# The turned rows six partitions apart, and low-rank sums with the tokens as the stationary operand

## The chip, the cores and the metric

The kernel runs on one core of one Trainium2 chip. The metric is the time of one execution on the device in microseconds, the median of three runs. Below, TensorE multiplies matrices into PSUM, VectorE, ScalarE and GpSimd do elementwise work, and SyncE issues the DMAs.

## The reference

Three stages follow each other, for 4 batches of 768 tokens with 384 channels.

1. A complex linear recurrence per head (8 heads of 48 channels): `S = (a_re + i a_im) * S + k v`, with `a` cut to a magnitude of 0.999, and `y = q S_re`.
2. A first MoE: `u = x + V'(U'x)`, where U (768x32) and V (32x768) mix tokens with rank 32; then `u + relu(u @ w_ch1) @ w_ch2` with 1536 hidden channels.
3. A second MoE of the same size, whose `u` is `x + Re(FFT2(x))`, normalised per token.

```python
h = xt @ U @ V                      # xt: channels x tokens
u = x + h.transpose(0, 2, 1)
ch = np.maximum(u @ w_ch1, 0.0) @ w_ch2
return (u + ch).astype(np.float32)
```

## The kernel before

**Attention.** A batch is cut into 6 chunks of 128 tokens, numbered 0 to 23 over the four batches. A pair of chunks is loaded with channels on partitions, as 16 groups of 8 heads. VectorE and ScalarE form decays and phases there (the functions `squares` to `gains`), and `rotations` writes q and k, scaled and turned by their phases, into QK: 128 partitions of (channel group x, head h), with the real or imaginary part z and the third i of a head's 48 channels as free axes. For the scores the 96 rows of a head (16 x, 2 z, 3 i) must lie on 96 partitions. `move` (line 316) does this by DMA: six per chunk, each taking QK's 128 partitions for one (z, i) to 16 partitions of QT, which are neighbours (`QT[p0 : p0 + 16]`). From QT and QK TensorE then makes the scores (`scores`, L325), masked by VectorE (L328); the keys turned back by an identity product (`turned`, L332), copied by ScalarE with `by_head` (L335); the sums with the values (`summed`, L343), which give y and the running state; and x, the output of the stage.

**The low-rank mix.** `low_rank` (line 384) multiplies, for each chunk of tokens, U's 128x32 part, repeated four times to 128 columns (three rounded copies and one of what rounding leaves), as the stationary operand with x's 128 tokens by 384 channels as the moving one:

```python
T.matmul(zp, f32(ust[:, c].rearrange("p a r -> p (a r)")), xt[b, c], start=c == 0, stop=c == NC - 1)
```

Six of these add up to zp. ScalarE rounds it to zst (L1028), VectorE replaces 32 of its rows by what the rounding left (L1030). V is then the second factor, once towards u with channels on partitions (`mixed`, L415) and once straight onto the MoE's sums (`extra1`, L449). In the trace an f32 matmul stands as two records, and each has its own weight load.

**The MoE.** For each batch and half a batch (g), `first_product` makes hp for 12 groups of hidden channels (f), ScalarE and VectorE split relu(hp) into hh and hl, and the second product adds onto acc. In the program hp is numbered through: hp_0 opens batch 0, hp_24 batch 1, hp_48 batch 2.

**What sets the order.** The attention of all batches and the first MoE of batches 0 to 2 are written as streams of steps, each with an engine, a duration and what it waits for. `planned` merges them into one order per engine before the program runs, and that order is fixed. PLACES holds a number per kind of step and batch that moves it ahead or back. Where the planner sees TensorE idle it puts in `warm_up` matmuls on constants, 128x256 before hp_0 (L609) and 128x128 behind it (L612). `rank_words` prepares U and V from 64-bit words, `mixing` holds the low-rank steps, `moves` the moves, `word_loads` the MoE's weight loads, which share three staging buffers with the turned keys. All DMAs of these stand on SyncE's one queue, in the planner's order. From batch 3's first MoE on, the order is written by hand, with the Fourier stage beside it.

## Time and profile before

| what | value |
| --- | --- |
| median of 3 runs (lowest, highest) | 863.51 us (861.82, 863.71) |
| the profiled execution | 863.16 us, its span 861.4 us |
| TensorE, VectorE, ScalarE, GpSimd busy | 93%, 73%, 52%, 4% of the span |
| granted clock of TensorE, mean | 0.997 of full speed |
| bytes over DMA | 83.06 MB, mean 96 GB/s |

The busy share of an engine is over the whole span, so stages with other limits are mixed in it; times within the trace count from the start of the span. Fillers count as busy time of TensorE.

### The profile page before, as it was taken

How to read it: one execution, taken by the hardware profiler on the slowest of the kernel's cores; microseconds unless marked ns; L12 is line 12 of the kernel's file. 1: busy time of each engine (PE TensorE's matmuls, PEld its weight loads, DVE VectorE, ACT ScalarE, POOL GpSimd, SP SyncE). 2: the span in 40 equal slices, each digit the busy share in tenths (PEclk: the TensorE clock that was granted, in tenths of full speed). 3: DMA queues.
4: the chain of work that ended last, by engine and by line, in shares of the span. 5: the costliest groups of instructions: out<-in, count | busy, mean ns of one | idle time of the engine just before them, and what ended most of it. 6: DMA issues, size and time to landing. Idle time of an engine off the chain costs nothing.

```text
span 861.4 us, 17279 instructions
## 1 busy us (share of the span) xinstructions
PE 799.0 (93%) x6947; PEld 542.1 (63%) x6947; DVE 627.7 (73%) x1304; ACT 450.6 (52%) x845; POOL 36.1 (4%) x79
## 2 busy tenths in 40 slices
PE   0298999999899999999999999999999999999996
PEld 0187755567766677666776665666666666666663
DVE  6989689998779977988965846657485657645652
ACT  7976598798868679758733342142224123311210
POOL 1001000010000000000003200001010100000000
PEclk9999999999999999999999999999999999999999
DMA  9539933588392594359386120103010300000000
GB/s 357 68 67 127 299 108 95 136 160 197 71 200 89 140 201 112 120 125 187 84 133 222 47 74 1 38 1 102 1 47 1 101 29 1 29 1 28 1 29 32
DMA packets 47353, 83.06 MB, mean 96 GB/s; under 512 B 5600, under 2 KB 36576, under 8 KB 47264
## 3 DMA queue, kind: packets, MB, share of 16 engines
q1 hardware_dynamic: 45984, 77.94, 37.6%
q0 software_dynamic: 1280, 3.93, 1.4%
q8 instruction: 56, 0.92, 0.5%
q14 instruction: 33, 0.27, 0.1%
HBM read 53.39 MB, written 9.44 MB: 73 GB/s over the span
## 4 chain that ended last, share of the span: by engine, by line
PE 75%; ACT 12%; DVE 6%; DMA 4%; issue 2%; SPq 1%; DVEq 0%; ACTq 0%
PE acc L210 10%; PE acc L211 10%; PE hp L105 10%; PE hp L107 10%; PE hp L106 10%; PE acc L224 7%; PE sc L325 4%; PE y L343 3%; PE acc L1083 3%; DMA QT<-QK 3%; ACT ain L101 2%; ACT L97 2%; PE g L343 1%; ACT hh L201 1%; PE z L385 1%
## 5 line engine op out<-in xcount | busy, mean ns | idle before, releaser
L201 ACT ACTIVATE hh<-hp 128x384 f16<-128x384 f32 x192 | 93.5, 489 | 303.5 <-PE hp L107 295.3
L204 DVE SCALAR_TENSOR_TENSOR hl<-hp,hh 128x384 f16<-128x384 f32 x192 | 105.6, 554 | 134.5 <-ACT hh L201 133.7
L210 PE MATMUL acc<-w,hh 128*128 128x384 f16 x576 | 187.7, 326 | 3.6 <-ACT hh L201 3.4
L211 PE MATMUL acc<-w,hh 128*128 128x384 f16 x576 | 187.3, 326 | 0.0
L105 PE MATMUL hp<-u,w 128*128 128x384 f16 x288 | 94.6, 328 | 0.1
L107 PE MATMUL hp<-u,w 128*128 128x384 f16 x288 | 94.5, 328 | 0.0
L106 PE MATMUL hp<-u,w 128*128 128x384 f16 x288 | 94.5, 328 | 0.0
L105 PE MATMUL hp<-n,w 128*128 128x384 f16 x288 | 93.9, 326 | 0.0
L107 PE MATMUL hp<-n,w 128*128 128x384 f16 x288 | 93.9, 326 | 0.0
L106 PE MATMUL hp<-n,w 128*128 128x384 f16 x288 | 93.9, 326 | 0.0
L210 PEld LDWEIGHTS <-hh 128*128 128x128 f16 x576 | 56.3, 98 | 40.4 <-ACT hh L201 6.6
L105 PEld LDWEIGHTS <-w 128*128 128x128 f16 x576 | 56.5, 98 | 37.8 <-issue 0.5
L107 PEld LDWEIGHTS <-w 128*128 128x128 f16 x576 | 56.5, 98 | 37.6 <-issue 0.5
L106 PEld LDWEIGHTS <-w 128*128 128x128 f16 x576 | 56.5, 98 | 36.8 <-issue 0.7
L224 PE MATMUL acc<-w,hl 128*128 128x384 f16 x360 | 77.5, 326 | 0.0
L211 PEld LDWEIGHTS <-hh 128*128 128x128 f16 x576 | 56.4, 98 | 33.1 <-issue 0.4
L325 PE MATMUL sc<-QT 96*128 96x128 f32 x384 | 50.0, 284 | 10.6 <-DMA QT<-QK 9.8
L325 PEld LDWEIGHTS sc<-QT 96*128 96x128 f32 x384 | 47.1, 197 | 13.0 <-issue 11.7
L332 PE MATMUL kp<-ident,QK 128*128 128x128 f32 x120 | 19.8, 292 | 33.6 <-DVE QK L309 31.3
L224 PEld LDWEIGHTS <-hl 128*128 128x128 f16 x360 | 35.2, 98 | 23.6
L1083 PE MATMUL acc<-w,hl 128*128 128x384 f16 x216 | 48.6, 327 | 1.4 <-DVE hl L204 1.4
L97 ACT ACT_TABLE_LOAD x33 | 42.3, 1283 | 1.3 <-PEq L1752 0.7
(264 smaller groups left out, 1414.4 us busy)
## 6 DMA issues: line engine op xcount, KB each, us to landing
QT<-QK SPq DMA_DIRECT2D x144, 129.0 KB, 6.9
stw<-in_w_dram SPq DMA_DIRECT2D x48, 384.0 KB, 5.3
ain<-in_a_dram SPq DMA_DIRECT2D x12, 768.0 KB, 7.0
qkin<-in_qk_dram SPq DMA_DIRECT2D x12, 768.0 KB, 6.9
x1d<-x SPq DMA_DIRECT2D x24, 192.0 KB, 3.4
vin<-in_v_dram SPq DMA_DIRECT2D x18, 192.0 KB, 3.4
lo<-x1d SPq DMA_DIRECT2D x12, 192.0 KB, 3.7
out_dram<-lo SPq DMA_DIRECT2D x12, 192.0 KB, 2.0
```

The costliest lines, as they stand in the source:

```text
L97: ordered(lambda: A.preload_act_table_set(name))
L105: T.matmul(o, ah, bh, start=start, stop=False, skip_group_check=skip)
L106: T.matmul(o, ah, bl, start=False, stop=False, skip_group_check=skip)
L107: T.matmul(o, al, bh, start=False, stop=stop, skip_group_check=skip)
L201: A.activation(hh, hp, AF.Relu)
L204: V.scalar_tensor_tensor(out=hl, in0=hp, scalar=0.0, in1=whole_of(hh), op0=ALU.max, op1=ALU.subtract)
L210: T.matmul(acc[t], hh[:, TSS[t]], w[:, 0, 384:], start=f == 0, stop=False)
L211: T.matmul(acc[t], hh[:, TSS[t]], w[:, 1, 384:], start=False, stop=False)
L224: T.matmul(acc[t], hl[:, TSS[t]], wt[mi, f][:, 0, 384:], start=False, stop=last_step and mi == 1)
L325: T.matmul(ps[:, h, :], q[:, 128:256], q[:, :128], start=True, stop=True)
L343: T.matmul(out[p, hsl], l(h)[:, p], r[:, hsl], start=h == 0 and o + done == 0, stop=h == 7 and o + rest == len(ops) - 1, skip_group_check= ...
L1083: T.matmul(accs[t], hls[n][:, TSS[t]], wt[0, every[n][2]][:, 0, 384:], start=False, stop=False)
```

## The change

`move` sends a (z, i) to the partitions z*3 + i, z*3 + i + 6, and so on: 16 partitions six apart, so that a head's row is x*6 + z*3 + i. `by_head` writes the turned keys in the same row order. U is kept once, as 128x32 in f32, without the rounded copies; its copy on ScalarE moves 192 columns instead of 576, and VectorE's pass for the rest (L705) is gone. `low_rank` now holds the tokens (three 128x128 parts of x) in TensorE, and U's 32 columns move; the sums lie as channels by ranks (zt, 96 columns for three parts). `thrice` has ScalarE copy each part's 32 columns three times beside each other, and `ranks_turned` turns the three 128x96 parts back on TensorE. From there all goes on as before, with 96 rows in place of 128. The planner is given 0.62 instead of 1.0 for a move and 0.25 instead of 0.65 for a chunk's sum, and every number in PLACES is new, so that the order of the planned part is another.

```diff
@@ -314,8 +314,7 @@
         V.tensor_copy(QK[:, :, :, 256:258], ew[m][4][:, :, j : j + 1].unsqueeze(1).to_broadcast([128, 2, 3, 2]))
 
     def move(QT, QK, z, i):
-        p0 = z * 48 + i * 16
-        nc.sync.dma_start(QT[p0 : p0 + 16], QK[:, z, i, :])
+        nc.sync.dma_start(QT[z * 3 + i : 96 : 6], QK[:, z, i, :])
 
     halves = slice(0, 64), slice(64, 128)
 
@@ -332,7 +331,8 @@
             T.transpose(ps[:, i * 128 : (i + 1) * 128], QK[:, z, i, 128:256], ident)
 
     def by_head(ks, ps, z):
-        A.copy(ks[:, :768].rearrange("t (h z x) -> t h z x", h=8, z=2)[:, :, z, :], ps.rearrange("t (x h) -> t h x", h=8))
+        to = ks[:, :768].rearrange("t (h x z i) -> t z h i x", h=8, z=2, i=3)
+        A.copy(to[:, z], ps.rearrange("t (i x h) -> t h i x", i=3, h=8))
 
     def summed(out, ops, done=0, rest=0):
 
@@ -381,23 +381,35 @@
         for n, sign in enumerate((1.0, -1.0)):
             V.tensor_scalar(unread, f32(vst), sign, 0.0, ALU.mult, ALU.max, accum_out=stat("v", 0, n))
 
-    def low_rank(zp, b, c):
-        T.matmul(zp, f32(ust[:, c].rearrange("p a r -> p (a r)")), xt[b, c], start=c == 0, stop=c == NC - 1)
+    def low_rank(zt, b, c):
+        for k in range(3):
+            ks = slice(k * 128, (k + 1) * 128)
+            T.matmul(zt[:, k * 32 : (k + 1) * 32], xt[b, c][:, ks], ust[:, c], start=c + k == 0, stop=c == NC - 1, skip_group_check=True)
+
+    def thrice(zt, b):
+        zx = xpl[0].tile([128, 3, 3, 32], F32, tag="zx", name=f"zx{b}", bufs=1)
+        A.copy(zx, zt.rearrange("d (k r) -> d k r", k=3).unsqueeze(2).to_broadcast([128, 3, 3, 32]))
+        return zx
+
+    def ranks_turned(zp, zx):
+        for k in range(3):
+            x = zx[:, k].rearrange("d n r -> d (n r)")
+            T.matmul(zp[:96, k * 128 : (k + 1) * 128], x, ident, is_transpose=True, start=k == 0, stop=k == 2, skip_group_check=True)
 
     def prelim(b):
 
-        zp = bank(f"z{b}")[:, :DM]
+        zp = bank(f"z{b}")
         for c in range(NC):
-            low_rank(zp, b, c)
+            low_rank(zp[:, DM:], b, c)
             if c % 2:
                 yield
+        zx = thrice(zp[:, DM : DM + 96], b)
+        ranks_turned(zp, zx)
         z = xpl[0].tile([128, DM], F32R, tag="zst", name=f"zst{b}", bufs=2)
-        A.copy(z, zp)
-        V.tensor_tensor(z[64:96], zp[64:96], f32(z[64:96]), ALU.subtract)
+        A.copy(z[:96], zp[:96, :DM])
+        V.tensor_tensor(z[64:96], zp[64:96, :DM], f32(z[64:96]), ALU.subtract)
         zst[b] = z
         yield
-        if parts16[0]:
-            A.activation(zp, zp, AF.Square, accum_out=stat("z", b, 0))
 
     def tokens(xp, b, g, k):
         for t in range(3):
@@ -414,8 +426,8 @@
     def mixed(xp, b, g, k):
         T.matmul(
             xp,
-            zst[b][:, k * 128 : (k + 1) * 128],
-            vst[:, g * 384 : (g + 1) * 384],
+            zst[b][:96, k * 128 : (k + 1) * 128],
+            vst[:96, g * 384 : (g + 1) * 384],
             start=False,
             stop=True,
             skip_group_check=True,
@@ -441,12 +453,12 @@
         for k in range(3):
             piece(k)
             if k == 2 and g == 1 and parts16[0]:
-                A.activation(zst[b], f32(zst[b]), AF.Copy, scale=UP * WP[0] * WP[1])
+                A.activation(zst[b][:96], f32(zst[b][:96]), AF.Copy, scale=UP * WP[0] * WP[1])
             yield
 
     def extra1(b, g, t, acc):
         c = g * 3 + t
-        T.matmul(acc, vst[:, c * 128 : (c + 1) * 128], zst[b], start=False, stop=True)
+        T.matmul(acc, vst[:96, c * 128 : (c + 1) * 128], zst[b][:96], start=False, stop=True)
 
     def added(acc, x, scale):
         if parts16[0]:
@@ -484,39 +496,39 @@
             yield
 
     PLACES = {
-        "squares": (-31, 3, 8, 62, 65, -112, 112, -43, 6),
...
-        "mixing": (25,),
...
+        "squares": (-28, -2, 5, 56, 44, -172, 104, -43, 14),
...
+        "mixing": (20,),
...
         "positive_lows": (-4,),
...
     }
     def planned(streams, sizes):
 
@@ -690,7 +702,7 @@
         def rank_words(x):
             u = x == "u"
             n = 192 if u else 384
-            yield op("A", 0.35 if u else 0.45, f"{x}a", x, holds=[("x1", f"{x}l")])
+            yield op("A", 0.35 if u else 0.45, f"{x}a", x, holds=[("x1", "uh" if u else f"{x}l")])
             w = slot(f"wx{x}")[:, :n]
             steps = word_steps(words_of[x], w)
             steps[0][1]()
@@ -699,10 +711,8 @@
                 steps[k][1]()
             if u:
                 ur = w.rearrange("p (c r) -> p c r", c=NC)
-                yield op("A", 0.6, "uh", "uc")
-                A.copy(ust[:, :, 0:3, :], ur.unsqueeze(2).to_broadcast([128, NC, 3, 32]))
-                yield op("V", 0.3, "ul", "uh")
-                V.tensor_tensor(ust[:, :, 3, :], ur, f32(ust[:, :, 0, :]), ALU.subtract)
+                yield op("A", 0.4, "uh", "uc")
+                A.copy(ust, ur)
             else:
                 zs = slice(int(x[1]) * 384, int(x[1]) * 384 + 384)
                 yield op("A", 0.45, f"{x}h", f"{x}c")
@@ -913,7 +923,7 @@
                     if c > 2:
                         before += [f"y{c - 3}"] + ([f"fe{c - 3}"] if turned_too(c - 3) else [])
                     at_end = (z, i) == (1, 2)
-                    yield op("S", 1.0, f"qt{c}" if at_end else f"qt{c}.{z}{i}", *before)
+                    yield op("S", 0.62, f"qt{c}" if at_end else f"qt{c}.{z}{i}", *before)
                     if z == i == 0:
                         QTs[c] = qk_tile("QT", *divmod(c, NC))
                     move(QTs[c], QKs[c], z, i)
@@ -1015,24 +1025,26 @@
         def mixing(b):
             for c in range(NC):
                 n = b * NC + c
-                if b == 0:
-                    yield op("P", 0.65, f"z{n}", f"x{n}", "ul", holds=[("hid", "zs0")] if c == 0 else [])
-                else:
-                    yield op("P", 0.65, f"z{n}", f"x{n}", f"x{b * NC + NC - 1}", holds=[("ms", f"zs{b}")] if c == 0 else [])
+                ready = [f"x{n}", "uh"] if b == 0 else [f"x{n}", f"x{b * NC + NC - 1}"]
+                yield op("P", 0.25, f"z{n}", *ready, holds=[("hid" if b == 0 else "ms", f"zs{b}")] if c == 0 else [])
                 if c == 0:
-                    banks["z", b] = bank(f"z{b}", phid if b == 0 else pms)[:, :DM]
-                low_rank(banks["z", b], b, c)
-            zp = banks["z", b]
-            yield op("A", 0.42, f"zh{b}", f"z{b * NC + NC - 1}", *([f"ex{b - 2}.1.2"] if b > 1 else []))
+                    banks["z", b] = bank(f"z{b}", phid if b == 0 else pms)
+                low_rank(banks["z", b][:, DM:], b, c)
+            zp = banks["z", b][:96, :DM]
+            yield op("A", 0.4, f"zx{b}", f"z{b * NC + NC - 1}", *([f"zt{b - 1}"] if b else []))
+            zx = thrice(banks["z", b][:, DM : DM + 96], b)
+            yield op("P", 0.35, f"zt{b}", f"zx{b}", "ident")
+            ranks_turned(banks["z", b], zx)
+            yield op("A", 0.42, f"zh{b}", f"zt{b}", *([f"ex{b - 2}.1.2"] if b > 1 else []))
             z = zst[b] = xpl[0].tile([128, DM], F32R, tag="zst", name=f"zst{b}", bufs=2)
-            A.copy(z, zp)
+            A.copy(z[:96], zp)
             yield op("V", 0.5, f"zl{b}", f"zh{b}", "v0l", "v1l")
             V.tensor_tensor(z[64:96], zp[64:96], f32(z[64:96]), ALU.subtract)
             yield op("A", 0.55, f"zs{b}", f"zl{b}")
-            A.activation(zp, zp, AF.Square, accum_out=stat("z", b, 0))
+            A.activation(zp, zp, AF.Square, accum_out=stat("z", b, 0)[:96])
             if b < LATE:
                 yield op("A", 0.5, f"zsc{b}", *[f"mix{b}.{g}.{k}" for g in range(2) for k in range(3)])
-                A.activation(z, f32(z), AF.Copy, scale=UP * WP[0] * WP[1])
+                A.activation(z[:96], f32(z[:96]), AF.Copy, scale=UP * WP[0] * WP[1])
 
         def pieces(b, g, k):
             if (b, g) == (0, 0):
@@ -1476,7 +1488,7 @@
     halfpi = const("halfpi", [128, 1])
     least = const("least", [128, 1])
     most = const("most", [128, 1])
-    ust = const("ust", [128, NC, 4, 32], F32R)
+    ust = const("ust", [128, NC, 32])
     vst = const("vst", [128, S], F32R)
     G.memset(one, 1.0)
     G.memset(stats, 0.0)
```

**SyncE's queue, moves of chunks 2 to 5** (QT_2 to QT_5 are the chunks' tiles, stw_f_z a weight load of the first MoE). Before:

```order
L318 DMA QT_3_532<-QK_3_520 16x8x258 x6
L128 DMA stw_2_0_720<-in_w_dram 128x768
L128 DMA stw_2_1_724<-in_w_dram 128x768
L318 DMA QT_4_796<-QK_4_742 16x8x258 x6
L128 DMA stw_3_0_817<-in_w_dram 128x768
L128 DMA stw_3_1_822<-in_w_dram 128x768
L318 DMA QT_5_825<-QK_5_793 16x8x258 x6
```

And with the change:

```order
L317 DMA QT_3_674<-QK_3_483 16x8x258 x6
L128 DMA stw_2_0_806<-in_w_dram 128x768
L317 DMA QT_4_808<-QK_4_747 16x8x258 x6
L317 DMA QT_5_883<-QK_5_798 16x8x258 x2
L128 DMA stw_2_1_904<-in_w_dram 128x768
L317 DMA QT_5_883<-QK_5_798 16x8x258 x3
L128 DMA stw_3_0_946<-in_w_dram 128x768
L128 DMA stw_3_1_949<-in_w_dram 128x768
L317 DMA QT_5_883<-QK_5_798 16x8x258
```

One weight load has gone from ahead of chunk 4's moves to between chunk 5's, and the last move of chunk 5 stands behind two more.

**TensorE, the opening of batch 1's first MoE** (xp is u before its split, zst1 the low-rank result of batch 1, kp_12 the turned keys of chunk 12, hp_24 the first product). Before:

```order
L404 MATMUL xp_1_0_2_2740<-ident_81,x_8_2366 128x128
L415 MATMUL xp_1_0_2_2740<-vst_89,zst1_2667 128x384
L332 MATMUL kp_12_0_2750<-ident_81,QK2_0_2744 128x128 x3
L332 MATMUL kp_12_1_2757<-ident_81,QK2_0_2744 128x128 x3
L105 LDWEIGHTS w0_255
L105 MATMUL hp_24_2764<-u_1_0_0_2710,w0_255 128x384
```

And with the change (fillers left out):

```order
L416 MATMUL xp_1_0_2_2741<-ident_81,x_8_2400 128x128
L427 MATMUL xp_1_0_2_2741<-vst_89,zst1_2707 128x384
...
L105 LDWEIGHTS w0_252
L105 MATMUL hp_24_2767<-u_1_0_0_2739,w0_252 128x384
L106 LDWEIGHTS w0_252
L106 MATMUL hp_24_2767<-u_1_0_0_2739,w0_252 128x384
```

The key turns of chunk 12 no longer stand ahead of hp_24; they come behind later products.

**TensorE, the low-rank sums of batch 2** (z2; x_12 to x_17 are its chunks of tokens). Before:

```order
L385 MATMUL z2_4007<-x_12_3000,ust_88 128x384
L385 MATMUL z2_4007<-x_13_3133,ust_88 128x384
L385 MATMUL z2_4007<-x_14_3691,ust_88 128x384
L385 MATMUL z2_4007<-x_15_3767,ust_88 128x384
L385 MATMUL z2_4007<-x_16_3886,ust_88 128x384
L385 MATMUL z2_4007<-x_17_3999,ust_88 128x384
```

And with the change:

```order
L387 MATMUL z2_4084<-ust_88,x_12_3234 128x32 x3
L387 MATMUL z2_4084<-ust_88,x_13_3299 128x32 x3
L387 MATMUL z2_4084<-ust_88,x_14_3787 128x32 x3
L387 MATMUL z2_4084<-ust_88,x_15_3869 128x32 x3
L387 MATMUL z2_4084<-ust_88,x_16_3948 128x32 x3
L387 MATMUL z2_4084<-ust_88,x_17_4078 128x32 x3
...
L397 MATMUL z2_4084<-ident_81,zx2_4119 96x128 x3
```

Six matmuls of 384 columns have become eighteen of 32, and three turns come one product later.

## Rows read from the trace of the kernel before

**Rows 1.** The page: busy time of each engine, and TensorE's busy tenths in 40 slices.

```profile
PE 799.0 (93%) x6947; PEld 542.1 (63%) x6947; DVE 627.7 (73%) x1304; ACT 450.6 (52%) x845; POOL 36.1 (4%) x79
...
PE   0298999999899999999999999999999999999996
```

**Rows 2.** Busy time by stretch: from:to, length, engines' busy us, TensorE's clock, DMA.

```profile
0.00:40.00 40.00, 2.44 (x9) 1.65 (x9) 31.80 (x55) 34.27 (x53) 2.21 (x15) 1.00 0.70 219
40.00:108.40 68.40, 63.40 (x864) 54.77 (x865) 56.14 (x95) 44.02 (x83) 4.22 (x10) 1.00 0.79 165
108.40:238.30 129.90, 121.87 (x1248) 84.98 (x1246) 115.22 (x188) 112.72 (x192) 3.25 (x12) 1.00 0.54 129
238.30:463.50 225.20, 223.45 (x2220) 155.26 (x2219) 183.41 (x312) 153.90 (x279) 10.75 (x24) 0.99 0.64 140
463.50:861.40 397.90, 387.81 (x2613) 245.46 (x2612) 241.09 (x657) 105.73 (x241) 15.64 (x18) 1.00 0.11 37
```

**Rows 3.** The chain that ended last, from 78 us on: start, us, what.

```profile
78.79 0.97 DVE QK L309
...
88.40 8.94 DMA QT<-QK
...
97.43 2.02 PE sc L325 x16
```

**Rows 4.** SyncE's queue from 79 us on: start, us, what it issued.

```profile
79.78 3.80 SPq L318 DMA_DIRECT2D QT<-QK  x6
83.69 1.02 SPq L128 DMA_DIRECT2D stw<-in_w_dram  x2
84.81 4.14 SPq L318 DMA_DIRECT2D QT<-QK  x6
```

**Rows 5.** The tile QT: its DMA issues (ns, min/median/max) and their time to landing.

```profile
L318 SPq DMA_DIRECT2D QT<-QK x144: 547/596/1492, 31.4 to 439.7; - x144
...
DMA to landing us min/median/max: 3.1/6.9/9.6
```

**Rows 6.** Stretches with moves alone, and with loads into 128 partitions; the last number is GB/s.

```profile
37.00:39.00 2.00, 0.00 (x0) 0.00 (x0) 1.90 (x3) 1.99 (x2) 0.00 (x0) 1.00 1.15 124
...
14.00:18.00 4.00, 0.00 (x0) 0.00 (x0) 3.00 (x5) 3.89 (x5) 0.00 (x0) 1.00 1.05 393
```

**Rows 7.** The chain again: scores of four heads, y, one batch's sums, key turns.

```profile
261.29 0.89 PE sc L325 x8
...
326.35 0.93 PE y L343 x32
...
337.38 3.87 PE z L385 x12
...
354.08 0.66 PE kp L332 x6
```

**Rows 8.** Groups of instructions by line: out<-in, shapes, count, busy us, mean ns, idle before.

```profile
L97 ACT ACT_TABLE_LOAD x33 | 42.3, 1283 | 1.3 <-PEq L1752 0.7
...
L609 PE MATMUL warm<-ident,mask 128*128 128x256 f16 x210 | 25.6, 281 | 0.0
...
L343 PEld LDWEIGHTS y<-S,QT 96*64 96x64 f32 x640 | 20.3, 138 | 5.3 <-issue 1.8 <-DVE pm L328 1.0 <-DVE wxw L139 0.5
...
L335 ACT COPY k<-kp 128x384 f32<-128x384 f32 x40 | 17.6, 477 | 11.5 <-PE kp L332 8.4 <-PE g L343 3.0
...
L612 PE MATMUL acc<-ident,mask 128*128 128x128 f16 x127 | 8.2, 219 | 0.0
...
L385 PEld LDWEIGHTS z<-x,ust 128*128 128x128 f32 x48 | 8.5, 190 | 4.2
...
L1327 ACT ACTIVATE ach<-ac 97x388 f16<-97x388 f32 x8 | 4.8, 598 | 0.0
```

**Rows 9.** TensorE in order of time before batch 1's first product; idle time in brackets.

```profile
237.49 1.00 PE L332 MATMUL kp<-ident,QK 128*128 128x128 f32 x6 [0.70 <-DVE QK L314]
238.29 0.52 PE L105 MATMUL hp<-u,w 128*128 128x384 f16 x1
```

60 lines of the change are left out of this document (30 added, 30 removed).

## The prediction

> **What bounds the kernel now.** I began with the page: TensorE is busy 799 us of 861.4, and its row of slices is empty only at the start [rows 1]. That busy time holds fillers, matmuls that the planner puts into gaps it foresees: 210 of 25.6 us and 127 of 8.2 us [rows 8]. So I cut the span at three events: the first product of the first MoE (108.4), the first product of batch 1 (238.3) and the first product of batch 3 (463.5), and read each stretch's busy time [rows 2]. Before 40 us TensorE works for 2.4 us. From 40 to 108.4 it is busy for 63.4, of which the 25.6 us of wide fillers are no work. From 108.4 to 238.3 it is busy for 121.9 of 129.9 (8.2 of it narrow fillers), while VectorE is busy for 115.2 and ScalarE for 112.7: all three are nearly full. After 238.3 TensorE idles 1.8 us in 225.2, and then 10.1 in 397.9, most of that at the very end. So up to 238.3 the elementwise work and the transfers set the pace, and behind it TensorE alone. The change acts on both sides, and I price them apart.
>
> **The moves.** Six transfers per chunk carry the turned rows into QT. In the chain of waits that ends last, chunk 5's rotation ends at 79.76, its last move starts landing behind others at 88.40 for 8.94 us, and its scores start at 97.43 [rows 3]. SyncE issues chunk 4's six moves from 79.78, two weight loads at 83.69, chunk 5's six from 84.81 [rows 4]. An issue takes 596 ns at the median, and the fastest move landed 3.1 us after its issue [rows 5]. Where moves run alone they bring 124 GB/s; loads into all 128 partitions bring 393 [rows 6]. One move is 16 x 8 x 258 x 4 = 132,096 bytes, so 132,096 / 124 GB/s = 1.06 us each: twelve need 12.8 us, and they queue behind each other. The change leaves bytes and count as they are and puts a move's 16 partitions six apart instead of side by side. The new time has no row. Above stands today's 1.06; below stands the issue, 0.60, for SyncE cannot hand out moves faster. I take 0.65, near the lower end: the only thing that sets the moves apart from the loads of 393 GB/s is that they end in 16 neighbouring partitions, and that is what is changed.
> [...]
> From the first issue of chunk 4 to the last landing of chunk 5 it is 97.34 - 79.78 = 17.6 us. With the new order (three weight loads among the moves, 0.5 us of issue each by [rows 4]): 12 x 0.65 + 3 x 0.5 + (3.1 - 0.6) = 11.8. **Saved: 5.8.** I take off 0.4, because the last move of chunk 5 now stands on SyncE's queue behind two weight loads that wait for buffers which TensorE frees; whoever is late there delays that move and the scores behind it.
>
> **The chain after the scores.** Behind the last low-rank sum two steps are added before U's product can be copied: ScalarE's threefold copy of 96 columns (no row for its 288 elements a lane; above stands the 0.48 of a 128x384 copy [rows 8], below three quarters of that by its elements, 0.36, and I take 0.45) and three turns, which by the six of 0.66 us [rows 7] cost 0.33. With a hop that is 0.9 us on the path of batch 0, so the first product starts 5.8 - 0.4 - 0.9 = **4.5 us earlier**. The rounding of U loses one vector pass and the copy to ScalarE shrinks; both run beside the first load of angles and I count nothing for them. ScalarE's key copies write a finer stride. They cost 477 ns [rows 8], and the nearest row with a strided store is 598 for as many elements a lane; I take 477, since these copies already read with a stride, and keep 40 x 0.12 = 4.8 us, spread over the attention, for the range. If that cover is gone, it is ScalarE's 113 of 130 us that fill up.
>
> **From 108.4 to 238.3.** The order has two table loads fewer between the first and the 25th product, 2 x 1.28 = 2.6 us off ScalarE [rows 8]. Since that stretch is limited by ScalarE and VectorE in turns I count the 2.6. At its end the product of batch 1 stood behind six key turns of chunk 12, which waited 0.7 us for a rotation and took until 238.29 [rows 9]: some 1.5 us, and in the new order these turns come two products later. Against this the copy and the turns are exposed once more (0.9), because batch 1's sums stand in one block with nothing behind them. Net 0.6. So batch 1 starts 4.5 + 2.6 + 0.6 = **7.7 us earlier**.
>
> **Behind 238.3, where every column counts.** One batch's sums, six chunks, are 12 records of 128 weights by 384 columns, 3.87 us [rows 7]. The new form has 18 matmuls, 36 records, each with its own load of a 128x128 f32 tile and only 32 moving columns. The trace has no such shape. Below: two neighbouring 64-wide halves of y run side by side, 32 records in 0.93 us, 29 ns each [rows 7], so 36 x 0.029 = 1.0 us. Above: the scores load 128 columns of f32 per record, as here, and take 0.89 / 8 = 0.112 us each, so 36 x 0.112 = 4.0 us. I take 4.0. The reason is in the loads' own times [rows 8]: 190 ns for 128 f32 columns, 138 for 64, 52 ns more for 64 columns, that is 0.8 ns a column. By that rate a 64-wide load holds its half for some 52 ns, and y's pairs come every 58 ns; a 128-wide load holds the whole array for some 104, and the scores come every 112. Both spacings then follow the loads, and fewer moving columns do not help.
> [...]
> So the batches 2 and 3 cost 2 x (4.0 - 3.87 + 0.33 for the turns) = 0.9 us more. The order also has 20 narrow fillers behind batch 1's first product where there were none, 20 x 8.2 / 127 = 1.3. **Together 2.2 us later.** The 96 instead of 128 rows of the products with V change no column, so nothing.
>
> **Sum.** -7.7 + 2.2 = -5.5 us. The profiled execution took 863.16 us (span 861.4 and 1.8 around it), so 857.7; the median of the three runs, 863.51, is 0.35 above it, so **858**.
>
> **Rivals.** First, the sums turn out light: the weight loads overlap as y's do, and the 32 columns set the time. For it: y's 29 ns per record. Against: those are halves of the array. Each batch is then up to 36 x (0.112 - 0.029) = 3.0 us shorter than I count, batch 1's on its exposed chain too; three batches give up to 9.0, and since y's pairs may flatter I say 8: **850**. Chance 0.25.
> Second, the start is not paced by the moves. Once chunk 5 lands earlier, VectorE and ScalarE, which already fill 56.1 and 44.0 of 68.4 us [rows 2] and are bunched towards the end of it, hold the first product where it is; the long rows of fillers around chunk 2's key turns (89 and 90 in the new order, 179 x 25.6 / 210 = 21.8 us) keep TensorE from catching up. It decides if chunk 5's scores start less than 2 us earlier. Then nothing of 4.5 and 2.6 is earned, the two exposed chains cost 1.8, the tail 2.2: with the key turns of chunk 12 out of the way (1.5) that is 863.5 + 1.8 + 2.2 - 1.5 = 866.0, and the fillers, if they end after the masks could have begun, add about 1: **867**, slower. Chance 0.15.
> Third, the change does not do what it says: a move six partitions apart still takes 1.06 us, being limited by 128 short packets and not by where they end. For it: 1,032-byte rows are the shortest of the large transfers. Then the start gains nothing and pays 0.9 for the longer chain and about 1.0 for the third weight load among the moves, the middle gives 3.2, the tail costs 2.2: +0.9, and the batches behind, whose order counts on short moves, may lose about as much again: **865**. Chance 0.10.
>
> **The numbers.** The forecast has 0.50. Its own range is 852 to 864: the moves at 0.60 or 0.85, the key copies at either end, the table loads earned twice or not at all. A measurement of this kernel tells about 0.2% (1.7 us) from no change. The light case is faster throughout; of the forecast's 0.50 some 0.42 lie below 861.8, 0.06 within, 0.02 above; the other two, 0.25 together, lie above but for 0.01 below and 0.07 within. Faster 0.68, same 0.13, slower 0.19. The range from 848 to 866 takes in the light case, the forecast and half of the other two.
>
> **What would show it.** Right: moves alone at 200 GB/s or more; chunk 5's scores near 91 to 92 us, the first product near 104, batch 1's near 230.5; 36 records of z in about 4 us, with VectorE's busy share behind 238 no lower. Wrong: 36 records in 1 to 2 us (first rival); moves at 125 GB/s (third); moves faster and the first product still at 107 or later (second). If batch 1's product comes at 230 and the end has not moved with it, TensorE idles after it for VectorE, which then has the work that the new order put off.

## The result, and the profile after

The changed kernel is **slower**: 875.22 us (median of 4 runs, 874.35 to 876.64) against 862.66 us for the kernel before (median of 4 runs on the same chip, 861.77 to 863.71). The ratio is 1.0137, with a 95% interval of 1.0098 to 1.0175. The forecast was 858 us, and its range ended at 866. The profiled execution took 876.64 us, its span 874.9.

The page of the changed kernel, its busy time of each engine, TensorE's busy tenths and its granted clock in 40 slices:

```profile
PE 810.6 (93%) x7075; PEld 559.8 (64%) x7075; DVE 628.0 (72%) x1303; ACT 457.5 (52%) x845; POOL 36.7 (4%) x79
...
PE   0499889999899999999999999999999999999996
...
PEclk9999699999999999999999999999999999999999
```

The busy share of TensorE is the same 93% as before [rows 1] in a longer span. What stands out is a 6 in the row of the clock, in the slice from 87 to 109 us. The same five stretches as before [rows 2], cut at the same events, show where the time went:

```profile
0.00:40.00 40.00, 5.35 (x22) 4.58 (x23) 32.47 (x56) 34.72 (x54) 3.51 (x17) 1.00 0.65 233
40.00:111.10 71.10, 68.30 (x901) 62.03 (x901) 54.24 (x88) 47.21 (x83) 3.64 (x8) 0.90 0.45 141
111.10:242.60 131.50, 122.15 (x1245) 86.39 (x1246) 108.98 (x182) 110.37 (x188) 3.04 (x10) 0.99 0.48 136
242.60:476.60 234.00, 226.95 (x2301) 161.23 (x2298) 191.15 (x323) 159.48 (x282) 11.60 (x27) 1.00 0.49 137
476.60:874.90 398.30, 387.88 (x2614) 245.56 (x2612) 241.18 (x658) 105.76 (x242) 14.94 (x18) 1.00 0.10 35
```

The first product comes at 111.1, 2.7 us later and not 4.5 earlier; batch 1's at 242.6, where 230.5 was forecast. The stretch between them is 1.6 us longer, the next one 8.8 us; from batch 3 on 0.4 us is all that differs. In the fourth stretch TensorE is idle for 234.0 - 226.95 = 7.05 us, where it was idle for 1.8 before.

**A move became as short as forecast, the way to chunk 5's scores did not.** The tile QT, its issues and the time to landing, and SyncE's queue from 76 us on (first and last of the entries for chunks 4 and 5):

```profile
L317 SPq DMA_DIRECT2D QT<-QK x144: 546/597/1387, 31.1 to 450.0; - x144
...
DMA to landing us min/median/max: 2.3/3.7/10.5
```

```profile
76.66 5.12 SPq L317 DMA_DIRECT2D QT<-QK  x8
...
86.45 0.56 SPq L317 DMA_DIRECT2D QT<-QK  x1
```

The issues cost what they did [rows 5]; the median landing fell from 6.9 to 3.7 us. Chunk 5's scores start at 93.19 in place of 97.43 [rows 3], 4.2 us earlier, but not by the sum of the prediction. From chunk 4's first issue to chunk 5's scores it is 93.19 - 76.66 = 16.5 us, where it was 97.43 - 79.78 = 17.7 and the prediction had 11.8 to the last landing: the last move is issued at 86.45, and its last packets end only at 92.3 in the trace, while the DMA engines are full with other loads (320 to 394 GB/s from 88 to 96 us, below). Most of the 4.2 us, 3.1, is the first issue itself, at 76.66 in place of 79.78. What follows the scores in the chain of waits reads ("issue" is time in which TensorE waited for nothing that the profile names):

```profile
91.54 1.65 issue
93.19 3.75 PE sc L324 x16
96.95 1.88 PE y L343 x32
```

The same 16 records took 2.02 us before [rows 3]. TensorE's busy time and granted clock in that place (from:to, length, busy, records, clock, DMA share, GB/s):

```profile
88.00:90.00 2.00, 2.00 (x42) 1.00 1.05 343
90.00:92.00 2.00, 0.95 (x10) 1.00 0.96 320
92.00:94.00 2.00, 0.81 (x4) 0.77 1.02 394
94.00:96.00 2.00, 2.00 (x11) 0.50 1.00 393
96.00:104.00 8.00, 8.00 (x84) 0.50 0.56 223
104.00:106.00 2.00, 2.00 (x12) 0.50 0.00 0
106.00:108.00 2.00, 2.00 (x17) 0.81 0.63 197
```

From about 93 to 107 us TensorE ran at 0.50, and the work between chunk 5's scores and the first product took longer (the 32 records of y behind the scores 1.88 us, where the kernel before took 1.07). So the 4.2 us are gone again before the first product. An estimate that bounds this for a whole run: the 16 records of the scores took 3.75 us at 0.50 and 2.02 at 1.00, so a microsecond at 0.50 does about half a microsecond's work, and a mean clock of c over the span costs at most some (1 - c) x span. That is 0.012 x 874.9 = 10.5 us here, against 0.003 x 861.4 = 2.6 in the profiled execution of before.

**The key copies did not do what was forecast.** Line L335 (count, ns as min/median/max):

```profile
L335 ACT COPY k<-kp x40: 826/874/945, 40.3 to 455.9; 128x384 f32<-128x384 f32 x40
```

They took 477 [rows 8]. **The sums took the forecast time on the engines**: 36 records of batch 2, then their turns, and the copy on ScalarE between them:

```profile
350.40 4.10 PE L387 MATMUL z<-ust,x 128*128 128x32 f32 x36
...
356.29 0.49 PE L397 MATMUL z<-ident,zx 128*96 128x128 f32 x3
...
354.54 0.40 ACT L391 COPY zx<-z 128x288 f32<-128x288 f32 x1 [3.39 <-PE z L387]
```

### The profile page after: what moved, and what is told of

Read it like the earlier page. It is cut to its first block, busy times and chain, and to the rows that moved or that the text cites. A ratio compares the mean times of both kernels' runs of the same rounds, so it can differ in the third digit from the quotient of the medians.

```text
span 874.9 us, 17544 instructions
## 1 busy us (share of the span) xinstructions
PE 810.6 (93%) x7075; PEld 559.8 (64%) x7075; DVE 628.0 (72%) x1303; ACT 457.5 (52%) x845; POOL 36.7 (4%) x79
## 4 chain that ended last, share of the span: by engine, by line
PE 73%; ACT 9%; DVE 8%; DMA 7%; issue 2%; SPq 1%; ACTq 0%; DVEq 0%
PE acc L210 9%; PE hp L105 9%; PE acc L211 9%; PE hp L107 9%; PE hp L106 9%; PE acc L224 7%; PE y L343 4%; PE sc L324 4%; DMA ain<-in_a_dram 3%; PE warm L621 3%; PE acc L1095 2%; PE z L387 2%; DMA QT<-QK 2%; DMA stw<-in_w_dram 2%; PE g L343 1%
## 5 line engine op out<-in xcount | busy, mean ns | idle before, releaser
L324 PE MATMUL sc<-QT 96*128 96x128 f32 x384 | 53.5, 293 | 8.4 <-DMA QT<-QK 5.3
L324 PEld LDWEIGHTS sc<-QT 96*128 96x128 f32 x384 | 49.2, 203 | 11.1 <-issue 7.5
L139 DVE SCALAR_TENSOR_TENSOR wxw<-wxw,stw 128x384 int32<-128x384 int32 x48 | 26.1, 553 | 18.2 <-ACT wxw L123 17.3
```

The costliest lines, as they stand in the source:

```text
L324: T.matmul(ps[:, h, :], q[:, 128:256], q[:, :128], start=True, stop=True)
```

## The experiments

All ratios are to the kernel before, measured beside each run on the same chip, where its median lay between 862.66 and 864.17 us; "clock" is the median over the runs of the mean granted clock. By the intervals a difference of two ratios is uncertain by 0.003 to 0.005, that is 2.6 to 4.3 us. In e1 and e4 the columns of the keys stand in another order than the rows of QT, so that they compute something else; they serve for prices alone.

| run | what it is | time, us | ratio (95%) | clock |
| --- | --- | --- | --- | --- |
| before | | 862.66 | 1 | 0.997 |
| after | all of the change | 875.22 | 1.0137 (1.0098 to 1.0175) | 0.989 |
| e1 | after, key copies as before | 873.81 | 1.0132 (1.0088 to 1.0177) | 0.990 |
| e2 | after, moves and copies as before | 916.98 | 1.0610 (1.0573 to 1.0648) | 0.965 |
| e3 | before + moves + copies | 857.12 | 0.9932 (0.9905 to 0.9958) | 0.998 |
| e4 | before + moves | 854.42 | 0.9894 (0.9867 to 0.9920) | 0.997 |
| e5 | before + moves + copies + sums | 862.79 | 0.9980 (0.9954 to 1.0005) | 0.994 |
| e6 | after, sums as before | 870.53 | 1.0068 (1.0042 to 1.0095) | 0.996 |
| e7 | after, fillers ahead of chunk 5 | 876.31 | 1.0122 (1.0080 to 1.0165) | 0.988 |
| e8 | before + moves, keys by head | 977.19 | 1.1290 (1.1244 to 1.1336) | 0.933 |
| e9 | after, fillers in both gaps | 877.68 | 1.0164 (1.0132 to 1.0196) | 0.987 |
| e10 | after, later landing in the plan | 881.90 | 1.0203 (1.0160 to 1.0246) | 0.984 |
| e11 | e9 and e10 | 880.71 | 1.0192 (1.0151 to 1.0233) | 0.989 |
| e12 | e3, copies in runs of 3 | 853.81 | 0.9881 (0.9854 to 0.9908) | 0.998 |
| e13 | e12 + extra sums, new shape | 869.40 | 1.0074 (1.0051 to 1.0097) | 0.993 |
| e14 | e12 + extra sums, old shape | 863.98 | 1.0011 (0.9992 to 1.0029) | 0.998 |
| e15 | e12 + sums | 860.27 | 0.9955 (0.9929 to 0.9981) | 0.993 |
| e16 | e6, copies in runs of 3 | 867.64 | 1.0065 (1.0037 to 1.0093) | 0.995 |

### Moves and key copies, in either order (e1 to e4)

The first question was whether moves and copies or the order make the change slow, so each was undone in the new order (e1, e2) and done alone in the old one (e3, e4); in all four the sequence of instructions on every engine stays that of the kernel they start from. The edits are one line or two:

```diff
 e1, e2: in by_head
+        A.copy(ks[:, :768].rearrange("t (h z x) -> t h z x", h=8, z=2)[:, :, z, :], ps.rearrange("t (x h) -> t h x", h=8))
 e2: in move
+        p0 = z * 48 + i * 16
+        nc.sync.dma_start(QT[p0 : p0 + 16], QK[:, z, i, :])
 e3, e4: in move of the kernel before (e3 with the new by_head as well)
+        nc.sync.dma_start(QT[z * 3 + i : 96 : 6], QK[:, z, i, :])
```

> The changed kernel with ScalarE's key copies storing their columns side by side again; moves, sums and order as changed. Left out: the columns of the keys then stand in another order than the rows of the turned tile, so the products with the state mix other rows; every instruction but these 40 copies is the same. Theory K (the stride of the key copies): a copy takes 874 ns at the median in the changed kernel and 479 before, 40 x 0.395 = 15.8 us of ScalarE, 12 of them behind the first product, and TensorE waits for ScalarE's hh there; a copy falls to 0.48 us, the 6.8 us lost between the 25th and the 49th product come back, time 866 to 869. Theory O (the order: VectorE's and ScalarE's steps stand at other places): the copies get shorter and the same wait shows up behind another step, time 873 to 876. The first product stays at 110 to 112 under both, for TensorE's clock at half speed ahead of it is not touched.

> The changed kernel with the moves into 16 neighbouring partitions and the key copies side by side again; the low-rank sums and the order as changed. Theory K: the key copies cost about 7 us and the moves gave chunk 5's scores 4.2 us that half clock ate again, so the first product stays within 2 us of 111, and the time is 866 to 870. Theory O: the order foresees short moves, so long ones cost the 4.2 us of chunk 5 and more behind it, time 877 to 884.

> The kernel before with its moves spread over 96 partitions and the key copies that go with them; low-rank sums, planner and order as before. Theory K: moves land sooner and chunk 5's scores start 3 to 5 us earlier, fillers that stand ahead of them keep the clock up, so the first product is 2 to 4 us earlier; the copies add 15.8 us of ScalarE, and 3 to 7 of these come back as waits of TensorE: 860 to 868. Theory O: nothing of the slowdown lies in moves or copies, time 856 to 860.

> The kernel before with its moves spread over 96 partitions and nothing else changed. Left out: the keys' columns keep their old order, so that the products with the state mix other rows. If the moves paced the start, as I forecast: chunk 5's scores 4 to 5 us earlier, first product 2 to 4 us earlier, time 857 to 860. If the start is not paced by them (the second rival of the prediction): first product at 107 to 109, time 861 to 864. Against the run with moves and copies this one gives the price of the copies' stride in the old order: theory K 3 to 7 us, theory O under 1.

In e1 a copy took 478 ns again, and the time stayed at 873.8, so theory K falls: the copies are not what slows the new order. In the old order the moves alone gave 1 - 0.9894, 1.06% or 9.1 us, more than either theory expected; chunk 5's scores start at 91.8 and the first product at 102.7, 5.6 and 5.7 us earlier than before. That is close to the 5.8 of the prediction, but not for its reasons. Chunk 4's moves on SyncE's queue in e4, and chunk 5's scores in the chain of waits:

```profile
75.86 3.79 SPq L317 DMA_DIRECT2D QT<-QK  x6
...
91.80 1.98 PE sc L324 x16
```

The prediction put all of the gain between chunk 4's first issue and chunk 5's scores. There e4 needs 91.80 - 75.86 = 15.9 us in place of 17.7, only 1.7 less; the other 3.9 us are the earlier first issue, 75.86 in place of 79.78, for which the prediction counted nothing. The rate it took was right: from 61 to 66 us, where moves run alone, e4 brings 200 GB/s, so 132,096 / 200 GB/s = 0.66 us a move.

The copies' stride takes 0.9932 - 0.9894 = 0.0038 of the gain back, 3.3 us. So e3 lies where theory O put it, and the price of the stride in the old order where theory K had it. Both expectations for e2 were far too small: the new order with long moves takes 917 us, with the first product at 129.3 and a mean clock of 0.79 from 40 to there. The new order has no slack for long moves; at most 0.035 x 916 = 32 us of its time are the lower clock.

### The sums and the order apart (e5, e6)

e5 takes the old PLACES and the old costs, and issues the copy and the turns inside the step of the copy that follows; e6 keeps the new order and puts the old sums into its steps.

```diff
 e5: in mixing
+            yield op("A", 0.42, f"zh{b}", f"z{b * NC + NC - 1}", *([f"ex{b - 2}.1.2"] if b > 1 else []))
+            zx = thrice(banks["z", b][:, DM : DM + 96], b)
+            ranks_turned(banks["z", b], zx)
 e6: in low_rank, with ust in four parts again and the steps zx and zt left empty
+        T.matmul(zp, f32(ust[:, c].rearrange("p a r -> p (a r)")), xt[b, c], start=c == 0, stop=c == NC - 1)
```

> All three parts of the change (moves, key copies, low-rank sums) in the order of before: old table of places, old costs, U's vector pass left as an empty step, and copy and turns of the sums issued in the step of the copy that follows them. Beside the run with moves and copies in the old order (857.1) it gives the price of the new sums alone. Theory O (the new order makes the change slow): the sums cost what the prediction's terms say, 0.9 us of longer chain in batches 0 and 1 and 0.5 to 0.9 in the two others, 858 to 861. Theory L (the new sums make it slow): 866 to 875.

> The changed kernel, its moves, copies and order kept, with the old low-rank sums (U's 128 columns held, the tokens moving; no copy, no turns; U's vector pass back). The other half of the same question: theory O, the time stays at 870 to 876 and the 25th to 49th product still lose 5 to 8 us; theory L, 857 to 863.

Theory O holds for the larger part: e6 lies in its range, and the new order costs 1.0068 - 0.9932 = 0.0136, 11.7 us, with nothing of the new sums in it. e5 lies between the two theories. The sums cost 0.9980 - 0.9932 = 0.0048, 4.1 us in the old order, and 1.0137 - 1.0068 = 0.0069, 6.0 us in the new one, where the prediction's terms make 0.9 in each of the batches 0 and 1 and 0.9 for the two others, 2.7; with the uncertainty above, neither difference alone is clear of 2.7. The four parts, -9.1 + 3.3 + 4.1 + 11.7, make +10.0 us; measured are +11.8.

In the new order most of the sums' price lies at the start: the first product of e6 comes at 104.8, that of the changed kernel at 111.1, which is 6.3 of the 8.3 us between the two profiled executions. Where the changed kernel ran at 0.50, e6 keeps its clock:

```profile
96.00:104.00 8.00, 7.60 (x82) 1.00 0.82 316
```

Its gaps there are also shorter (0.59 us in all from 88 to 92), so this alone does not tell the new sums from the gaps.

**Where the order loses.** e3 and e6 have the same moves, copies and sums. Their stretches from the first product of batch 0 to those of batches 1, 2 and 3 (engines in the order TensorE, its loads, VectorE, ScalarE, GpSimd), e3:

```profile
102.60:234.90 132.30, 121.90 (x1247) 84.98 (x1246) 115.08 (x188) 115.82 (x192) 2.92 (x12) 1.00 0.44 126
234.90:345.20 110.30, 109.72 (x1109) 76.98 (x1108) 94.39 (x158) 89.75 (x154) 1.45 (x9) 1.00 0.51 141
345.20:457.60 112.40, 111.79 (x1114) 77.64 (x1113) 88.76 (x154) 70.59 (x126) 7.37 (x15) 1.00 0.49 144
```

and e6:

```profile
104.80:234.50 129.70, 120.25 (x1218) 83.55 (x1219) 109.07 (x182) 110.08 (x188) 3.37 (x10) 1.00 0.49 138
234.50:353.30 118.80, 114.21 (x1135) 78.84 (x1133) 98.98 (x167) 88.64 (x154) 2.07 (x11) 1.00 0.48 129
353.30:468.40 115.10, 112.11 (x1117) 77.99 (x1115) 92.14 (x159) 69.44 (x127) 9.70 (x16) 1.00 0.50 145
```

The new order does 6.0 us less of VectorE's work ahead of batch 1's first product (109.07 against 115.08) and 4.6 and 3.4 us more in the two stretches behind it. Its first product comes 2.2 us later, the three stretches are -2.6, +8.5 and +2.7 us longer, and the clock is 1.00 in all of them. In the middle one TensorE is idle for 4.6 us in place of 0.6; the rest of the 8.5 is longer busy time, 1 to 2 us of it fillers. What holds the stretch up is told by the chain of waits that ends last, in shares by line, over the middle stretch of e3 and of e6:

```profile
by line: PE acc L210 11.3%; PE acc L1083 10.9%; PE hp L105 10.7%; PE hp L107 10.6%; PE hp L106 10.6%; PE acc L211 10.6%; PE y L343 10.3%; PE sc L324 9.9%; PE g L343 4.7%; PE z L385 3.5%; PE kp L331 2.8%; PE xp L404 1.8%; PE xp L415 0.9%; PE
```

```profile
by line: DMA ain<-in_a_dram 13.5%; PE acc L210 7.2%; PE hp L105 7.1%; PE hp L107 7.0%; PE hp L106 7.0%; PE acc L1082 6.8%; PE acc L211 6.6%; PE sc L324 5.1%; PE y L343 4.4%; PE z L385 3.3%; issue 2.9%; PE g L343 2.8%; DMA stw<-in_w_dram 2.7
```

In e3 TensorE is its own bound there, as [rows 2] had shown for the kernel before. In e6 the chain runs through the loads of angles. The waits of ScalarE and of TensorE's loads in e6 name them (who waits, for whom, us in all, times, longest):

```profile
ACT ls L737 <- DMA ain<-in_a_dram: 4.5, 2, 2.3
...
PEld L210 <- ACT hh L201: 4.4, 6, 1.3
```

A load of angles is issued when the rotations of an earlier pair have freed its buffer. With the rotations later, the load is later, ScalarE stands waiting for it, and the hh behind that step on ScalarE's queue keeps TensorE waiting (in e3 its loads wait 1.0 us for hh there). This is read from the trace; no run changes it alone. Another candidate is left untested too: the new plan counts 0.25 us for a chunk's sum, where the trace has 4.1 / 6 = 0.68 with the new sums and 3.87 / 6 = 0.65 with the old ones.

### Two attempts to mend the new order (e7, e9 to e11), and one to mend the copies (e8, e12)

```diff
 e7: in score_steps
+                if c == 5 and hf == 0:
+                    warm_up(2.2, True)
 e9: 1.4 there, and in mixing ahead of chunk 4's sums
+                if n == 4:
+                    warm_up(0.9, True)
 e10: in planned
+                done[label], done[label + " issued"] = free["Q"] + (2.3 if label in ('a8', 'a9', 'a10') else 0.3), t + 0.6
```

> The changed kernel with 20 more wide fillers right ahead of chunk 5's scores, where TensorE idles 2.2 of 3.1 us and its granted clock then reads 0.50 from 94 to 106. Theory C (that half clock eats the 4 us that the moves gained): the clock reads 1.0 there, chunk 5's scores to the first product take 11 to 13 us in place of 17.9, the first product comes at 104 to 107; the time falls by as much if what follows keeps the lead (869 to 871), or by 1 or less if VectorE and ScalarE hold batch 1 where it is (874 to 875). If the clock is not what holds the first product: it stays at 110 or later.

> The changed kernel with 8 wide fillers ahead of the low-rank sums of chunk 4 and 12 ahead of chunk 5's scores, that is in the two gaps (0.59 and 1.65 us) behind which the granted clock fell; the run with 20 fillers in the second place brought the clock back at 96, but the fillers themselves ran at half clock and held the scores until 96.4. Theory C: the clock stays at 1.0 through the stretch, chunk 5's scores start at 93 to 94, the first product at 105 to 107, 4 to 6 us earlier than in the changed kernel. If the start passes on to the end: 868 to 872. If VectorE and ScalarE, which have work put off in the new order, take the lead back before batch 1: 874 to 877.

> The changed kernel with one number of its plan nearer to the trace: the landing of three loads of angles (chunk pairs 8, 9 and 10, which land 7.6, 7.3 and 8.2 us after their issue, where the plan foresees 5.5) is counted 2.0 us later, and the order of all that follows comes out of the plan again. Theory W (TensorE waits in batch 1 for ScalarE's hh, which stands behind a step that waits for these loads): first product of batch 1 as before, to that of batch 2 it takes 113 to 117 us in place of 119.5, time 868 to 873. Rival: the loads are only the last of a chain that is late as a whole (rotations some 16 us later than in the old order), so another step waits in their place: 874 to 877.

> The fillers in the two gaps and the later landing in the plan together. If both losses are separate and pass on: 863 to 868. If the chain of VectorE and ScalarE in batch 0 and 1 takes either back: 872 to 877.

e7: the fillers came into the half clock themselves (0.51 from 92 to 94), so the scores started at 96.4; from there to the first product, at 108.8, it took 12.4 us, as expected, but at 876.3 neither total was met. e9 did in its profiled execution what it was made for: the clock reads 1.00 from 88 to the first product, which comes at 105.2, 5.9 us earlier, and the end is 3.9 us earlier (span 871.0). Yet this was its shortest run, at a mean clock of 0.992; the five others, at 0.985 to 0.991, took 876 to 882. The profile of e9 already shows where the clock can fall instead: 0.58 from 110 to 114, behind a gap of more than 2 us, and 0.83 on the mean of 228 to 238 and of 344 to 354, around the sums of batches 1 and 2. So half clock at the start was a real loss and not the only place for it. Since e9 keeps the new sums there and only fills the gaps, the gaps have a share in the fall at the start; whether they would do it without the new sums is not shown. e10 missed: 881.9. The plan answered the later landing with 72 more narrow fillers (197 in place of 125), so it changed more than the loads, and nothing follows on them. e11 has the same fault.

The key copies could be mended. e8 lays heads side by side; e12 only changes the loop order, so that the three columns that lie side by side are stored one after another:

```diff
 e8: in by_head and keyed
+        to = ks[:, :768].rearrange("t (x z i h) -> t z i x h", z=2, i=3, h=8)
+        A.copy(to[:, z], ps.rearrange("t (i x h) -> t i x h", i=3, h=8))
+        return [(lambda h: ks[:, h:768:8], vin)]
 e12: in by_head of e3
+        A.copy(to[:, z].rearrange("t h i x -> t h x i"), ps.rearrange("t (i x h) -> t h x i", i=3, h=8))
```

> The kernel before with the moves spread and the key copies laid out so that the 8 heads lie side by side in source and store (runs of 8 in place of a stride of 6); the products of the keys then load every 8th column, 96 of them in two loads of 64 and 32. Same order as before. Theory: a copy takes 0.5 us or less, so the time is that of moves alone, 853 to 857. Rival: columns 32 bytes apart make the weight loads of these products slower, and 20 groups of 32 loads cost TensorE more than the copies cost ScalarE: 860 to 868.

> The kernel before with the moves spread and the key copies in another loop order: the three columns of a run innermost (3 side by side in the store, then the next run 24 bytes on) in place of 16 columns 24 bytes apart. Everything else as in the run with moves and copies in the old order, 857.1. If the price of a copy is in stores that leave the run they were in: 0.5 to 0.7 us a copy, 854 to 856. If it goes by the stride of the outer loop: 0.87 again, 857. Rival: a read 512 bytes apart innermost costs more than it saves, over 0.9, 858 to 861.

e8 missed by a hundred microseconds, though its copies take 479 ns, as many as before. Its products of the keys (g), and below them those of the kernel before:

```profile
L344 PE MATMUL g<-vin,k 128*64 128x48 f32 x320 | 71.8, 311 | 0.3 <-ACT k L335 0.3
...
L344 PE MATMUL g<-vin,k 128*32 128x48 f32 x320 | 54.4, 258 | 0.0
...
L344 PEld LDWEIGHTS g<-vin,k 128*64 128x64 f32 x320 | 50.5, 206 | 13.8 <-issue 1.8 <-ACT k L335 1.0 <-ACT ain L780 0.6
```

```profile
L343 PE MATMUL g<-vin,k 128*64 128x48 f32 x640 | 22.6, 224 | 0.3 <-ACT k L335 0.3
...
L343 PEld LDWEIGHTS g<-vin,k 128*64 128x64 f32 x640 | 20.4, 138 | 4.2 <-issue 2.4 <-ACT k L335 0.8 <-ACT w L163 0.3
```

The same 640 products keep TensorE busy for 71.8 + 54.4 = 126.2 us in place of 22.6; that is 103.6 of the 977.2 - 854.4 = 122.8 us that e8 is slower than e4, which has the same moves. A load of 64 columns takes 206 ns in place of 138, and so do on the mean the 230 of the 320 that ran wholly at a clock of 1.00. The records also overlap far less (before, 640 of 224 ns pass in 22.6 us; here 320 of 311 ns need 71.8); whether that is the stride or the new split into 64 and 32 columns is not told apart. Part of the time is the clock, 0.933 over the run, at most 0.067 x 975 = 65 us. The rival had the right sign and far too small a size. e12 works:

```profile
L335 ACT COPY k<-kp x40: 534/561/582, 43.5 to 422.4; 128x384 f32<-128x384 f32 x40
```

That is 561 ns in place of 874, and **853.81 us, 0.9881 of the kernel before (0.9854 to 0.9908): faster than both kernels.**

### Does the shape of the new sums lower the clock? (e13 to e16)

Every kernel with the new sums has a median clock of 0.994 or less; every one with the old sums, e8 with its slow loads apart, 0.995 or more. To tell the shape from the gaps around it, 36 more records of the new shape were put ahead of the sums of batches 1, 2 and 3 in e12, or 12 of the old one, for the same time on TensorE. Nothing waits for them.

```diff
 e13: in mixing of e12, once ahead of each batch's sums
+                    for x in range(NC if b else 0):
+                        for k in range(3):
+                            T.matmul(whole[:, DM + k * 32 : DM + (k + 1) * 32], xt[b, x][:, k * 128 : (k + 1) * 128], f32(ust[:, x, 0]), start=x + k == 0, stop=x == NC - 1, skip_group_check=True)
 e14: the same loop with
+                        low_rank(banks["z", b], b, x)
```

> The run with copies in runs of 3 (old order, old sums, 853.8, granted clock 0.996 to 0.999), with 18 more matmuls ahead of the sums of batches 1, 2 and 3 in the shape of the new sums: 128 columns of tokens held, U's 32 columns moving, into unread columns of the same bank. Nothing waits for them. Both theories: 3 x 4.0 us more on TensorE, 865.8. Theory S (the shape itself lets the clock fall though TensorE has no gap): the mean granted clock reads 0.994 or less, a stretch at 0.50 begins during or right behind such a block, time 868 to 876. Rival (the clock falls only because of gaps ahead of and behind the sums): clock 0.996 to 0.999, 864 to 867.

> The same place and nearly the same time on TensorE in the old shape: the 6 matmuls of the old sums (U's 128 columns held, 384 columns of tokens moving) done twice in batches 1, 2 and 3. Both theories: 3 x 3.9 us more, the clock stays at 0.996 to 0.999, 864 to 867. It is the control for the run with the new shape; if the clock falls here as well, neither theory stands.

TensorE in order of time in e13, and then its busy time and clock around the same block:

```profile
332.32 0.33 PE L107 MATMUL hp<-u,w 128*128 128x384 f16 x1
332.48 4.10 PE L1027 MATMUL z<-ust,x 128*128 128x32 f32 x36
336.42 5.81 PE L385 MATMUL z<-x,ust 128*128 128x384 f32 x12
```

```profile
332.00:334.00 2.00, 2.00 (x19) 1.00 0.92 269
334.00:336.00 2.00, 2.00 (x21) 1.00 0.08 30
336.00:338.00 2.00, 2.00 (x9) 0.73 0.00 0
338.00:340.00 2.00, 2.00 (x5) 0.50 0.00 0
340.00:342.00 2.00, 2.00 (x7) 0.92 0.04 8
```

TensorE has no gap: it is busy for 2.00 of every 2.00 us, comes from full products and goes on with the old sums. Still the clock falls to 0.50 right behind the 36 records, and the old sums take 5.81 us where they take 3.87 at full clock [rows 7]. It falls so in all three batches (0.83 on the mean of 219 to 229, 332 to 342 and 455 to 465). In e14 the three blocks read:

```profile
220.00:228.00 8.00, 8.00 (x32) 1.00 0.08 25
330.00:338.00 8.00, 8.00 (x29) 1.00 0.24 75
452.00:460.00 8.00, 8.00 (x28) 1.00 0.85 266
```

Theory S holds: without a gap, the shape alone can bring the clock down. e13 is 1.0074 - 1.0011 = 0.0063, 5.4 us, slower than its control, of which the three blocks' own times explain 3 x (4.0 - 3.87) = 0.4; its clock is 0.005 lower, at most 4.3 us, and what is left is within the uncertainty. Its eleven runs follow the clock, from 865.7 us at 0.996 to 871.4 at 0.990.

It does not do so behind every such block. In the changed kernel itself the 36 records of batches 1, 2 and 3 start at 234.1, 350.4 and 466.0, and its profiled execution reads at their ends:

```profile
236.00:240.00 4.00, 3.51 (x39) 1.00 0.80 248
352.00:356.00 4.00, 4.00 (x34) 1.00 0.01 4
468.00:472.00 4.00, 4.00 (x33) 1.00 0.86 257
```

In the profiled executions of e5 and e15 the clock falls at one and at two of the three blocks (e5: 0.50 from 230 to 232; e15: 0.50 from 226 to 232 and from 454 to 460). What decides it was not found.

> All parts of the change in the order of before (862.8, clock 0.986 to 0.997), with the key copies in runs of 3. The copies gave 3.3 us beside the old sums (857.1 to 853.8). If that adds: 859 to 861, with the clock as low as it was; the gap to 853.8 is then the price of the new sums, clock included.

> The new order with the old sums (870.5), with the key copies in runs of 3, 561 ns in place of 874: 12 us less of ScalarE. Theory O (the order itself is slow: one pair of chunks less of VectorE's attention work stands ahead of batch 1's first product, and TensorE waits behind it): 866 to 870. Rival (the order is slow because it counts a key copy at 0.42 us and ScalarE falls behind): 857 to 862.

e15 is e5 and e16 is e6, each with the loop order of e12. Both came out as expected. e15, all of the change in the old order with mended copies, takes 860.3: the sums cost 0.9955 - 0.9881 = 0.0074, 6.4 us, with a clock that is 0.0055 lower, at most 4.7 of them. e16 takes 867.6: with the copies mended the new order still costs 0.0184, 15.9 us, so it is not slow for what ScalarE's copies cost.

## Why the prediction was wrong

The prediction failed in two steps: it took the bound of the old order for that of the new one, and it priced the new sums by their durations alone.

**"Behind 238.3, where every column counts."** That TensorE alone sets the pace there was read from rows of the old order [rows 2] and carried over to the new one. The rows were right for the old order: in e3 the chain is TensorE's. In the new order it is not: batches 1 and 2 take 234.0 us where they took 225.2 and 227.4 were forecast, with TensorE idle for 7.05 in place of 1.8. The order costs 11.7 us (e6 against e3), nearly all of it behind batch 1's first product, where the prediction counted 1.3 for fillers. The last sentence of the prediction named the sign to look for, that TensorE idles behind batch 1's product for work the new order put off; it stood there as a doubt and had no price. The stretch before it, with 2.6 us for two table loads and 0.6 net, brought nothing in the changed kernel: it became 1.6 us longer, and ScalarE has 11 table loads in it where it had 12. What in the new order makes the rotations late was not settled: the later rotations and the waits for the loads are read from the trace, and the one run that was meant to test them (e10) changed the order as a whole.

**"Two batches cost 2 x (4.0 - 3.87 + 0.33) more", and the 0.9 for the chain.** The durations held: 36 records in some 4.0 us, a copy of 0.40 against 0.45 forecast, turns of 0.49 to 0.53 against 0.33. But the term had no clock in it. The sums were worth 2.7 us by it and cost 4.1 to 6.4 by three pairs of runs, and that their shape can lower TensorE's clock is shown by e13 against e14 (0.50 behind three blocks of three, against 1.00). In the profiled execution of the changed kernel the clock fell behind none of the batches 1 to 3, but at the start, where chunk 4's new sums stand between the gaps of 0.59 and 1.65 us ahead of chunk 5's scores (what share each has was not told apart); there the half clock ate the whole gain of the moves.

Right was the price of a move: 0.65 us were taken, and 0.66 follow from the 200 GB/s of e4. That chunk 5's scores came 5.6 us earlier in e4, close to the 5.8 forecast, is luck: 1.7 came in the stretch that the sum described and 3.9 ahead of it. The sum had the weight loads among the moves at 0.5 us of issue each and nothing for their bytes; by [rows 6], 393,216 bytes at 393 GB/s are an estimate of 1.0 us each on the same DMA engines. At the end e4 gains 9.1 us; batch 1's first product is 5.5 earlier, batch 3's 8.7, and where the gain between them comes from was not followed up (in the profiled execution of before the clock reads 0.57 from 238 to 242).

The key copies were left at 477 ns, with 4.8 us of ScalarE kept for the range. They took 874, which is 15.9 us of ScalarE, 3.3 of them on the path in the old order. The nearest row with a strided store, 598 ns, had been taken as the upper end, and the copies went far beyond it. The store has 48 columns side by side before, 8 in e8, 3 in e12 and 1 in the change, and a copy took 479, 479, 561 and 874 ns.

Of the rivals, light sums did not come (4.1 us a batch). "A start that the moves don't pace" alone forecast a slower kernel beyond the noise, 867, but its condition did not hold: chunk 5's scores start 4.2 us earlier, not less than 2, and in e4 the lead reaches the first product. A move is not bound by its packets either: their landing fell to 3.7 us.

## What to carry to other kernels

Price a change of the order as a change of its own: run the edit in the old order first, since prices read from the old order tell nothing of the waits in a new one. Where the rows say that elementwise work and matmuls are nearly level, see whether the new order moves work of the other engines behind the point from which TensorE was alone. And matmuls with few moving columns can cost more than their durations (the three blocks of 36 made e13 5.4 us slower than e14, where their own times explain 0.4): read the granted clock behind them, with a control of equal length in another shape, and in more than one execution.

## What the runs showed of the hardware that was not expected

- TensorE's granted clock fell from 1.00 to 0.50 right behind 36 records of 128 held by 32 moving f32 columns, with TensorE busy for 2.00 of 2.00 us all along, in three blocks of three (e13); behind 24 records with 384 moving columns it did not, in three of three (e14). In the profiled execution of the changed kernel it did not fall behind any of three such blocks of 36.
- Weight loads of f32 columns 32 bytes apart took 206 ns for 64 columns in place of 138 (e8); the 640 products with them, split into 64 and 32 columns in place of 64 and 64, kept TensorE busy for 126.2 us in place of 22.6.
- ScalarE's copy of 128x384 f32 from PSUM took 479, 561 or 874 ns with 48 (or 8), 3 or 1 columns side by side in the store.
- Transfers of 132 KB into 16 partitions landed in 3.3 us at the median with the partitions six apart (e4), and in 6.9 side by side; alone they brought 200 GB/s against 124.
